# Loads and constants of an attention kernel's opening put in another order

## The chip, the cores and the metric

The kernel runs on one core of a Trainium2 chip. The metric is the device time of one execution in microseconds (us). Engines are named as the profile names them: PE is TensorE (PEld its weight loads), DVE is VectorE, ACT is ScalarE, POOL is GpSimd, SP is SyncE; SPq and ACTq are the queues on which SP and ACT issue transfers (DMAs).

## The reference: sparse attention, then two mixtures of experts

```python
scores = scale * np.matmul(q, k.transpose(0, 1, 3, 2))      # q, k, v: 2 x 8 heads x 576 x 64
kth = np.partition(scores, -top_k, axis=-1)[..., -top_k:-top_k + 1]      # top_k = 32
scores = np.where(scores >= kth, scores, -1e9)
attn = softmax(scores)
x = heads side by side of attn @ v                          # 1152 x 512
x = moe(x, w_gate, w1, w2, capacity)                        # 8 experts, 512 -> 1024 -> 512, best expert of each token
return moe2(x, w_gate, w1, w2)
```

## The kernel before: how the work is staged

Attention comes first and lasts to about 240 us; the two mixtures of experts follow. Attention works through eight units, each two heads of one batch, and each unit through nine tiles of 128 queries. For a tile PE makes the scores, ACT copies them to SBUF, and DVE looks for the 32nd largest score of each row (folds of maxima and minima, then MAX8 and MATCH_REPLACE8 in turn); then follow exponential and product with the values.

Products in full precision need each number in two parts. A unit's keys and queries are loaded (`kraw`, `qraw`), split into `ks` and `qs` (ACT copies the rounded part, DVE subtracts it from the raw number, POOL copies a third part of the keys), and turned by PE with a product against the identity matrix `identr`. For the first unit this is written out in `begin()`: the function `part_of` makes one copy and one subtraction, `whole` makes four transpositions, `wide_spin` and `spin` are products without use that keep PE busy. A unit's keys and queries have a main part (512 rows, as 128 partitions) and a tail (the last 64 rows). `begin()` asks for the main keys and queries of head 0, then both tails, then three groups of transpositions.

The identity matrices are made at the start of the kernel, in a block of constants: POOL writes a ramp `jp`, and DVE compares it with zero to give `ident`, `identr`, `negid`, `before` and `upto`. `coef` in the same block is a tile of three numbers; the first ACTIVATE of the kernel, on a tile `warm`, reads it and serves only to have ACT's function table loaded (ACT_TABLE_LOAD) early.

Each engine runs its own list of instructions in order. The block of constants and the attention are each written in an order by hand, but they are two blocks, and the builder merges them into one list for each engine: where a row of one stands beside rows of the other follows from the build. Waits between engines are semaphores set by the builder. Transfers are issued in order on SPq or ACTq.

Of the kernel before, what the change touches and what calls it, by code (L numbers as in the profile page):

```python
# [10 lines left out]
F32 = mybir.dt.float32  # L11
# [4 lines left out]
AF = mybir.ActivationFunctionType  # L16
# [9 lines left out]
BIG = 2.0 ** 80  # L26
# [28 lines left out]
def attn_moe_moe_kernel(ctx, tc, q, k, v, g1, w11, w12, capacity, g2, w21, w22, out):  # L55
    nc = tc.nc
    B, H, S, D = q.shape
# [4 lines left out]
    NC = (S + 127) // 128  # L62
    TAIL = S - (NC - 1) * 128
    cap = int(capacity)
    scale = 1.0 / math.sqrt(D)

    consts = ctx.enter_context(tc.tile_pool(name="consts", bufs=1))
    dram = ctx.enter_context(tc.tile_pool(name="dram", bufs=1, space=DR))
    first_w = ctx.enter_context(tc.tile_pool(name="mw1", bufs=1))

    with tc.manual_schedule():
        ones = consts.tile([128, 128], BF)
        nc.vector.memset(ones, 1.0)
        idle = consts.tile([128, 128], BF)
        nc.vector.memset(idle, 0.0)
        jp = consts.tile([128, 128], I32)
        nc.gpsimd.iota(jp, pattern=[[1, 128]], base=0, channel_multiplier=-1)
        ident = consts.tile([128, 128], F32)
        nc.vector.tensor_scalar(ident, jp, 0.0, None, op0=OP.is_equal)
        identr = consts.tile([128, 128], F32R)  # L80
        nc.vector.tensor_scalar(identr, jp, 0.0, None, op0=OP.is_equal)
        negid = consts.tile([128, 128], BF)
        nc.vector.tensor_scalar(negid, jp, 0.0, -1.0, op0=OP.is_equal, op1=OP.mult)
        coef = consts.tile([128, 3], F32)
        nc.vector.memset(coef[:, 0:1], -1.0)
        nc.vector.memset(coef[:, 1:2], BIG)
        nc.vector.memset(coef[:, 2:3], -scale)
        before = consts.tile([128, 128], BF)
        nc.vector.tensor_scalar(before, jp, 0.0, None, op0=OP.is_gt)
        upto = consts.tile([128, 128], BF)  # L90
        nc.vector.tensor_scalar(upto, jp, 0.0, None, op0=OP.is_ge)
# [100 lines left out]
    def attention():  # L192
# [4 lines left out]
        M = NC - 1  # L197
# [4 lines left out]
        with tc.tile_pool(name="ald", bufs=2) as ld, tc.tile_pool(name="awk", bufs=2) as wk, \  # L202
                tc.tile_pool(name="aps", bufs=1, space=PS) as ps, tc.manual_schedule():
            st = {}
            held_t = []
            for i in range(2):
                qt = wk.tile([128, 2, 192], F32R, name=f"qtail{i}", bufs=1)
                nc.gpsimd.memset(qt.bitcast(F32), 0.0)
                xl = wk.tile([128, NC, 2, XW], F32, name=f"xl{i}", bufs=1)
                vT = wk.tile([128, NC, 128], F32, name=f"vT{i}", bufs=1)  # L210
# [3 lines left out]
            shifted, under, vx = [], [], []  # L214
# [18 lines left out]
            xo = xb[:, :6 * XW].rearrange("p (g h w) -> p g h w", h=2, w=XW)  # L233
            zero = blank
            pend = []

            def load(u, what=("k", "q", "v"), eng=None):
                b, p = divmod(u, HP)
                z = st.setdefault(u, {"vT": held_t[u % 2][0], "xl": held_t[u % 2][1], "qtail": held_t[u % 2][2],
                                      "v": vx[u % 4]})  # L240
                dma = (eng or nc.sync).dma_start
                for nm in what:
                    s_ = {"k": k, "q": q, "v": v, "w": v}[nm][b, 2 * p:2 * p + 2]
                    if nm == "v":
                        if "vw" not in z:
                            load(u, ("w",))
                        for hh in range(2):
                            dma(z["v"][:, :M, hh, :D], s_[hh, :M * 128, :].rearrange("(s c) d -> s c d", s=128))
                        dma(z["v"][:TAIL, M, :, :D], s_[:, M * 128:, :].rearrange("h s d -> s h d"))
                    elif nm == "w":  # L250
                        t = z["vw"] = ld.tile([128, NC, 2, D], F32, name="vraw", bufs=2)
                        for hh in range(2):
                            dma(t[:, :M, hh], s_[hh, :M * 128, :].rearrange("(s c) d -> s c d", s=128))
                        dma(t[:TAIL, M], s_[:, M * 128:, :].rearrange("h s d -> s h d"))
                    else:
                        t = ld.tile([128, 2, NC, D], F32, name=nm + "raw", bufs=2)
                        if nm == "q":
                            for hh in range(2):
                                dma(t[:, hh, :M], s_[hh, :M * 128, :].rearrange("(c s) d -> s c d", s=128))
                        else:  # L260
                            dma(t[:, :, :M], s_[:, :M * 128, :].rearrange("h (s c) d -> s h c d", s=128))
                        dma(t[:TAIL, :, M], s_[:, M * 128:, :].rearrange("h s d -> s h d"))
                        z[nm] = t.rearrange("s h c d -> s c h d")
# [426 lines left out]
            def spin(n, o):  # L690
                for _ in range(n):
                    idle_product(o)
# [97 lines left out]
            seq = [(u, t) for u in range(NU) for t in order[u]]  # L790
            pairs = {}
            spin(17, xb[:, :256])
            load(0, ("k",))
            load(0, ("q",), nc.scalar)
            warm = wk.tile([128, 1], F32, name="warm", bufs=1)
            nc.scalar.activation(warm, coef[:, :1], AF.Exp)
            load(1, ("q",))
            load(0, ("w",))
            load(1, ("k",))
# [120 lines left out]
            for i in range(L - 4):  # L920
                k_, j_ = divmod(i, 2)
# [81 lines left out]
            z = st[u]  # L1003
# [13 lines left out]
            for c in range(NC):  # L1017
                w, k_ = c % 2, c // 2
# [1088 lines left out]
    rank_cuts = (0, 3, 6, 9, None)  # L2107
    w2_order = ((0, 1), (2, 3), (4, 5), (6, 7), (0, 1), (2,), (3, 4, 5, 6, 7))
    repair(attention())
    small = [ctx.enter_context(tc.tile_pool(name=f"msm{i}", bufs=1)) for i in range(2)]  # L2110
    onehot = small[0].tile([128, 128 * max(B * NC, NCOL + nov[0])], BF, name="onehot")
# [37 lines left out]
```

## Time and profile before

| | us |
|---|---|
| time before, median of 3 runs | 582.86 (582.47 to 583.42) |
| the profiled execution's own time | 583.19 |
| its span in the trace | 581.5 |
| PE busy | 566.0 (97%) |
| DVE busy | 475.5 (82%) |
| ACT busy | 419.4 (72%) |

The span is what the trace covers; 1.7 us of the execution's own time lie around it. The busy shares are means over stages with different limits: up to about 240 us DVE has no idle time to speak of, afterwards PE has none. "Idle before" in a row is the time that an engine stood still ahead of an instruction, with what ended it behind an arrow.

### The profile page before, as it was taken

The page shows a single profiled execution, that of the slowest core. Times are in us where ns is not written, and L with a number is a line of the kernel's source. Part 1 is how long each engine was busy: PE and PEld are TensorE (multiplying, and loading weights), DVE is VectorE, ACT ScalarE, POOL GpSimd, SP SyncE. Part 2 cuts the span into 40 slices and gives each one's busy share as a digit, 9 for nine tenths or more (in the row PEclk, how much of TensorE's full clock was granted, in tenths as well). Part 3 has the DMA queues.
Part 4 walks back from the last instruction along what each step waited for, and adds up shares of the span by engine and source line. Part 5 has one row for each costly group of instructions (what it writes and reads, how often), then busy time and mean ns, then how long its engine had stood idle before and what let it go on. Part 6 is the DMA issues. An engine that isn't in the chain of part 4 may idle for free. (4 is left out here: it accounts for less than half of the span.)

```text
span 581.5 us, 13994 instructions
## 1 busy us (share of the span) xinstructions
PE 566.0 (97%) x4786; PEld 539.2 (93%) x4786; DVE 475.5 (82%) x1588; ACT 419.4 (72%) x1040; POOL 267.1 (46%) x600
## 2 busy tenths in 40 slices
PE   8999999999999999989999999999999999999994
PEld 6799999999999999889999999998998899999993
DVE  6999999999999999868788788552588788889640
ACT  6789998999898988637687787452465677878550
POOL 8768888988898798546320111010103302220010
PEclk9999999999999999999999999999999999999998
DMA  6630513161211482055998767875777767678650
GB/s 145 143 83 2 169 46 114 45 127 43 70 48 62 70 254 77 23 196 181 349 280 282 221 227 250 287 236 198 237 253 244 278 232 260 225 249 298 211 203 14
DMA packets 85200, 100.76 MB, mean 173 GB/s; under 512 B 33957, under 2 KB 46757, under 8 KB 85120
## 3 DMA queue, kind: packets, MB, share of 16 engines
q1 hardware_dynamic: 79136, 86.69, 48.2%
q0 software_dynamic: 3728, 10.70, 5.4%
q10 hardware_dynamic: 2256, 2.39, 1.3%
q8 instruction: 40, 0.66, 0.5%
q14 instruction: 40, 0.33, 0.2%
HBM read 86.51 MB, written 13.74 MB: 172 GB/s over the span
## 5 line engine op out<-in xcount | busy, mean ns | idle before, releaser
L624 PE MATMUL xb<-vx,pT 128*128 128x73 f32 (+1 forms) x800 | 94.0, 266 | 0.2 <-ACT pT L1014 0.2
L1367 PE MATMUL pp<-xT,w1c 128*128 128x352 f32 (+4 forms) x316 | 92.4, 361 | 0.4 <-DVE xT L1323 0.4
L1288 DVE TENSOR_TENSOR w2c<-raw,w2c 128x512 fp32r<-128x512 f32 x112 | 74.5, 684 | 18.6 <-ACT w2c L1287 16.8
L624 PEld LDWEIGHTS xb<-vx,pT 128*128 128x128 f32 (+1 forms) x800 | 87.1, 181 | 2.5 <-issue 1.3
L1406 PE MATMUL pp<-hT,w2c 128*128 128x416 f32 (+4 forms) x320 | 88.7, 356 | 0.1
L1408 PE MATMUL pp<-hT,w2c 128*128 128x208 f32 (+4 forms) x320 | 77.8, 243 | 0.0
L1369 PE MATMUL pp<-xT,w1c 128*128 128x176 f32 (+4 forms) x316 | 77.0, 244 | 0.0
L1287 ACT ACTIVATE w2c<-raw 128x512 fp32r<-128x512 f32 x112 | 67.4, 624 | 8.7 <-PE pp L1408 3.7
L603 PE MATMUL pt<-ident,shifted 128*128 128x128 f32 x350 | 67.5, 278 | 0.0
L604 PE MATMUL pt<-negid,under 128*128 128x128 bf16 x350 | 63.5, 219 | 0.5 <-ACT under L594 0.5
L1288 DVE TENSOR_TENSOR w1c<-raw,w1c 128x512 fp32r<-128x512 f32 x88 | 55.9, 684 | 9.5 <-ACT w1c L1287 7.5
L1339 ACT ACTIVATE t<-pp 128x208 f32<-128x208 f32 (+4 forms) x120 | 37.6, 314 | 34.2 <-PE pp L1369 21.6
L1408 PEld LDWEIGHTS pp<-hT,w2c 128*128 128x128 f32 x320 | 61.0, 191 | 0.0
L1406 PEld LDWEIGHTS pp<-hT,w2c 128*128 128x128 f32 x320 | 60.0, 187 | 1.0 <-DVE hT L1333 0.8
L1367 PEld LDWEIGHTS pp<-xT,w1c 128*128 128x128 f32 x316 | 59.4, 188 | 1.4 <-DVE xT L1323 0.8
L1369 PEld LDWEIGHTS pp<-xT,w1c 128*128 128x128 f32 x316 | 60.4, 191 | 0.0
L1469 POOL DMA_INDIRECT out_dram<-yr,sidx x14 | 13.6, 972 | 101.1 <-ACT yr L1450 84.7
L594 ACT ACTIVATE under<-s,nb 128x576 bf16<-128x576 f32 x70 | 54.9, 786 | 1.5 <-POOL nb L586 1.3
L1792 POOL DMA_DIRECT2D y<-yr x13 | 7.6, 582 | 105.3 <-issue 45.1
L523 DVE MAX8 top<-ypair 128x8 f32<-128x160 f32 x192 | 54.7, 313 | 0.0
L597 POOL TENSOR_SCALAR shifted<-s,nb 128x576 f32<-128x576 f32 x70 | 52.3, 747 | 3.9
L603 PEld LDWEIGHTS pt<-ident,shifted 128*128 128x128 f32 x350 | 49.2, 140 | 3.6
(421 smaller groups left out, 1547.8 us busy)
## 6 DMA issues: line engine op xcount, KB each, us to landing
raw<-in_moe_w_dram SPq DMA_DIRECT2D x60, 1024.0 KB, 5.1
w1c<-in_moe_w_dram SPq DMA_DIRECT2D x8, 512.0 KB, 6.3
y<-blank SPq DMA_DIRECT2D x3, 769.5 KB
out_dram<-blank SPq DMA_DIRECT2D x3, 768.0 KB
y<-yr POOLq DMA_DIRECT2D x8, 256.5 KB
kraw<-in_k_dram SPq DMA_DIRECT2D x8, 256.0 KB, 3.4
vraw<-in_v_dram SPq DMA_DIRECT2D x16, 128.0 KB, 2.8
vx<-in_v_dram SPq DMA_DIRECT2D x16, 128.0 KB, 2.8
```

What stands on the lines that cost most here:

```text
L523: ops.append(lambda w=w, cur=cur: nc.vector.max(w, cur))
L594: nc.scalar.activation(under[k % 3][:, :S], s, AF.Relu, bias=nb[:, 1:2], scale=-BIG)
L597: nc.gpsimd.tensor_scalar(shifted[k % 3][:, :S], s, nb[:, 0:1], 1.0, op0=OP.add, op1=OP.mult)
L603: both = (nc.tensor.matmul(pt[:, o], shifted[k % 3][:, o], ident, is_transpose=True, start=True, stop=False), nc.tensor.matmul(pt[:, o], u ...
L604: nc.tensor.matmul(pt[:, o], under[k % 3][:, o], negid, start=False, stop=True))
L624: nc.tensor.matmul(o, pT[:, c2, cols], z["v"][:, c2, hh], start=(c2 == 0), stop=(c2 == NC - 1))
L1287: nc.scalar.activation(o[:, 0], src_, AF.Copy)
L1288: nc.vector.tensor_tensor(o[:, 1], src_, o[:, 0].bitcast(F32), op=OP.subtract)
L1367: nc.tensor.matmul(ph[:, :2 * n].rearrange("p (w n) -> p w n", w=2), w[f][:, 0, d], xT[:, d, :, :n], start=st, stop=False)
L1369: nc.tensor.matmul(ph[:, :n], w[f][:, 1, d], xT[:, d, 0, :n], start=False, stop=sp)
L1406: nc.tensor.matmul(py[:, :2 * n].rearrange("p (w n) -> p w n", w=2), w[f][:, 0, o], hT[:, f, :, :n], start=st, stop=False)
L1408: nc.tensor.matmul(py[:, :n], w[f][:, 1, o], hT[:, f, 0, :n], start=False, stop=sp)
```

## The change

Three things move. `coef` is written first in the block of constants. On ACT the function table's load stands behind one transfer's issue (the tail of the keys) in place of three (the queries of both heads and their tail). The first unit's transfers are shared out anew: SPq has the main keys, the main queries of head 0 and the tail of the queries, ACTq has the tail of the keys and, behind the table's load, the main queries of head 1.

```diff
     with tc.manual_schedule():
+        coef = consts.tile([128, 3], F32)
+        nc.vector.memset(coef[:, 0:1], -1.0)
+        nc.vector.memset(coef[:, 1:2], BIG)
+        nc.vector.memset(coef[:, 2:3], -scale)
         ones = consts.tile([128, 128], BF)
         nc.vector.memset(ones, 1.0)
...
         negid = consts.tile([128, 128], BF)
         nc.vector.tensor_scalar(negid, jp, 0.0, -1.0, op0=OP.is_equal, op1=OP.mult)
-        coef = consts.tile([128, 3], F32)
-        nc.vector.memset(coef[:, 0:1], -1.0)
-        nc.vector.memset(coef[:, 1:2], BIG)
-        nc.vector.memset(coef[:, 2:3], -scale)
...
+            def load_first(then):
+
+                z = st.setdefault(0, {"vT": held_t[0][0], "xl": held_t[0][1], "qtail": held_t[0][2], "v": vx[0]})
+                k_, q_ = k[0, :2], q[0, :2]
+                kt = ld.tile([128, 2, NC, D], F32, name="kraw", bufs=2)
+                qt = ld.tile([128, 2, NC, D], F32, name="qraw", bufs=2)
+                head = lambda hh: (qt[:, hh, :M], q_[hh, :M * 128, :].rearrange("(c s) d -> s c d", s=128))
+                tail = lambda t, s_: (t[:TAIL, :, M], s_[:, M * 128:, :].rearrange("h s d -> s h d"))
+                nc.sync.dma_start(kt[:, :, :M], k_[:, :M * 128, :].rearrange("h (s c) d -> s h c d", s=128))
+                nc.scalar.dma_start(*tail(kt, k_))
+                nc.sync.dma_start(*head(0))
+                then()
+                nc.sync.dma_start(*tail(qt, q_))
+                nc.scalar.dma_start(*head(1))
+                z["k"], z["q"] = (t.rearrange("s h c d -> s c h d") for t in (kt, qt))
...
-            load(0, ("k",))
-            load(0, ("q",), nc.scalar)
             warm = wk.tile([128, 1], F32, name="warm", bufs=1)
-            nc.scalar.activation(warm, coef[:, :1], AF.Exp)
+
+            def table_load():
+                nc.scalar.activation(warm, coef[:, :1], AF.Exp)
+
+            load_first(table_load)
             load(1, ("q",))
```

The built lists show more than the diff does. DVE's list of the kernel before, from the block of constants to the first unit's four first subtractions (128x4x64 is a main part of head 0, 64x2x64 a tail of both heads):

```order
L79 TENSOR_SCALAR ident<-jp 128x128
L81 TENSOR_SCALAR identr<-jp 128x128
L83 TENSOR_SCALAR negid<-jp 128x128
L85 MEMSET coef 128x1
L86 MEMSET coef 128x1
L87 MEMSET coef 128x1
L89 TENSOR_SCALAR before<-jp 128x128
L91 TENSOR_SCALAR upto<-jp 128x128
L717 TENSOR_TENSOR ks<-kraw,ks 128x4x64
L717 TENSOR_TENSOR qs<-qraw,qs 128x4x64
L717 TENSOR_TENSOR ks<-kraw,ks 64x2x64
L717 TENSOR_TENSOR qs<-qraw,qs 64x2x64
```

DVE's list of the changed kernel at the same place (its L733 is L717 of before):

```order
L75 MEMSET coef 128x1
L77 MEMSET ones 128x128
L79 MEMSET idle 128x64
L733 TENSOR_TENSOR ks<-kraw,ks 128x4x64
L733 TENSOR_TENSOR qs<-qraw,qs 128x4x64
L733 TENSOR_TENSOR ks<-kraw,ks 64x2x64
L733 TENSOR_TENSOR qs<-qraw,qs 64x2x64
L83 TENSOR_SCALAR ident<-jp 128x128
L85 TENSOR_SCALAR identr<-jp 128x128
L87 TENSOR_SCALAR negid<-jp 128x128
L89 TENSOR_SCALAR before<-jp 128x128
L91 TENSOR_SCALAR upto<-jp 128x128
```

The five comparisons that make `ident`, `identr`, `negid`, `before` and `upto` have moved from ahead of the four subtractions to behind them; no line of the diff says so.

ACT's list of the kernel before, from its first row:

```order
L259 DMA qraw<-in_q_dram 128x4x64 x2
L262 DMA qraw<-in_q_dram 64x2x64
L796 ACT_TABLE_LOAD
L796 ACTIVATE warm<-coef 128x1
L712 ACTIVATE ks<-kraw 128x4x64
L712 ACTIVATE qs<-qraw 128x4x64
L712 ACTIVATE ks<-kraw 64x2x64
L712 ACTIVATE qs<-qraw 64x2x64
```

ACT's list of the changed kernel at the same place:

```order
L246 DMA kraw<-in_k_dram 64x2x64
L812 ACT_TABLE_LOAD
L812 ACTIVATE warm<-coef 128x1
L250 DMA qraw<-in_q_dram 128x4x64
L728 ACTIVATE ks<-kraw 128x4x64
L728 ACTIVATE qs<-qraw 128x4x64
L728 ACTIVATE ks<-kraw 64x2x64
L728 ACTIVATE qs<-qraw 64x2x64
```

One issue stands ahead of the table's load where there were three, and one behind it. On SPq the list begins with the main keys in both kernels; before, the tail of the keys and unit 1's queries came next, and now two transfers of the first unit's queries stand ahead of unit 1's. PE's and POOL's lists keep their order.

## Rows read from the trace of the kernel before

**Rows 1.** Busy time by stretch: us, PE, PEld, DVE, ACT, POOL, granted clock, DMA.
```profile
0.00:10.00 10.00, 8.52 (x48) 6.04 (x48) 5.10 (x17) 5.63 (x14) 7.83 (x35) 1.00 0.74 150
10.00:20.00 10.00, 8.36 (x60) 6.36 (x60) 9.99 (x41) 6.94 (x16) 8.06 (x18) 1.00 0.66 154
...
180.00:200.00 20.00, 20.00 (x199) 19.26 (x198) 19.98 (x80) 18.49 (x46) 15.66 (x37) 1.00 0.47 95
...
300.00:400.00 100.00, 100.00 (x781) 97.37 (x780) 67.97 (x168) 64.56 (x165) 13.30 (x27) 1.00 0.79 253
```

**Rows 2.** DVE's waits, 9.6 to 60 us: total us, times, longest.
```profile
DVE hi L505 <- ACT s L478: 0.7, 2, 0.5
```

**Rows 3.** Timeline of DVE in the opening: start us, us, engine, line, operation.
```profile
1.26 0.41 DVE L79 TENSOR_SCALAR ident<-jp 128x128 f32<-128x128 int32 x1
1.40 0.34 DVE L81 TENSOR_SCALAR identr<-jp 128x128 fp32r<-128x128 int32 x1
...
4.54 0.43 DVE L717 TENSOR_TENSOR ks<-kraw,ks 128x256 fp32r<-128x256 f32 x1 [1.58 <-ACT ks L712]
...
6.22 0.28 DVE L717 TENSOR_TENSOR qs<-qraw,qs 64x128 fp32r<-64x128 f32 x1
...
9.60 0.31 DVE L505 TENSOR_TENSOR hi<-sc,s 128x144 f32<-128x144 f32 x1 [0.46 <-ACT s L478]
```

**Rows 4.** Timeline of PE in the opening.
```profile
1.25 3.79 PE L124 MATMUL xb<-idle,ones 128*128 128x256 bf16 x17 [1.25 <-DVE idle L75]
5.02 0.75 PE L285 MATMUL sc<-identr,ks 128*128 128x128 f32 x4
...
6.60 0.60 PE L124 MATMUL sc<-idle,ones 128*128 128x512 bf16 x2
7.14 0.25 PE L285 MATMUL xb<-identr,qs 64*128 64x64 f32 x1
...
8.27 0.54 PE L473 MATMUL pt<-qkT 128*128 128x288 f32 x2
```

**Rows 5.** Timeline of ACT in the opening.
```profile
0.85 1.07 ACTq L259 DMA_DIRECT2D qraw<-in_q_dram  x2
1.96 0.72 ACTq L262 DMA_DIRECT2D qraw<-in_q_dram  x1
2.71 1.28 ACT L796 ACT_TABLE_LOAD   x1 [2.71 <-issue]
4.00 0.20 ACT L796 ACTIVATE warm<-coef 128x1 f32<-128x1 f32 x1
4.11 0.40 ACT L712 ACTIVATE ks<-kraw 128x256 fp32r<-128x256 f32 x1
4.47 0.42 ACT L712 ACTIVATE qs<-qraw 128x256 fp32r<-128x256 f32 x1
5.45 0.31 ACT L712 ACTIVATE ks<-kraw 64x128 fp32r<-64x128 f32 x1 [0.56 <-DMA kraw<-in_k_dram]
5.72 0.31 ACT L712 ACTIVATE qs<-qraw 64x128 fp32r<-64x128 f32 x1
```

**Rows 6.** Timeline of SP's queue in the opening.
```profile
0.86 0.44 SPq L261 DMA_DIRECT2D kraw<-in_k_dram  x1
1.36 0.75 SPq L262 DMA_DIRECT2D kraw<-in_k_dram  x1
2.15 1.34 SPq L259 DMA_DIRECT2D qraw<-in_q_dram  x2
```

**Rows 7.** DMA issues, 0 to 30 us: KB each, median us from issue to landing.
```profile
qraw<-in_q_dram SPq DMA_DIRECT2D x6, 128.0 KB, 3.3
...
wg<-in_moe_w_gate_dram SPq DMA_DIRECT2D x2, 16.0 KB, 2.2
```

**Rows 8.** PE's products by shape in short stretches: count, busy us, mean ns.
```profile
L124 PE MATMUL xb<-idle,ones 128*128 128x256 bf16 x10 | 2.3, 421 | 0.0
...
L124 PE MATMUL sc<-idle,ones 128*128 128x512 bf16 x4 | 1.0, 382 | 0.0
```

## The prediction

> **What bounds the kernel now.** I read the busy time by stretch first [rows 1]. From 10 us on DVE is busy 9.99 of 10 us, and at 180 to 200 us still 19.98 of 20; from 300 us it is PE, 100 of 100. Between 0 and 10 us no engine is full: DVE has 5.10 us of work there. DVE's waits say the same: from 9.6 to 60 us it stands still for 0.7 us in all, and 0.46 of that is the wait for its very first fold [rows 2, 3]. So the opening is a chain of latencies that ends when DVE's first fold begins at 9.60, and after that DVE runs without a gap. Whatever moves 9.60 moves the rest of attention by the same amount, and what follows waits for attention's end.
>
> Second, the chain itself, followed back from 9.60. The fold waits for ACT's copies of the first scores; the scores start at 8.27 [rows 4]. Back from there PE has hardly a gap: tails turned from 7.14, idle products from 6.60, and the first transpositions from 5.02. These start 0.05 us after DVE's first subtraction (4.54 + 0.43 = 4.97) [rows 3], which waits for ACT's copy at 4.11, and that begins as soon as the table is loaded (2.71 to 3.99) and the small ACTIVATE on it is done [rows 5]. The 17 idle products fill PE from 1.25 to 5.04, so it has no gap. The identity is long there: `identr` ends at 1.40 + 0.34 = 1.74 [rows 3].
>
> **The change, part by part.** *The table's load.* ACT issues one tail in place of three transfers: 0.85 + 0.72 = 1.57, table from 1.60 to 2.88, small ACTIVATE to 3.09, then the queries of head 1 (half of 1.07, 0.54) to about 3.64. The first copy can start at 3.66 and not 4.11 [rows 5]: a gain of 0.45 us, if the keys have landed; before shows only that they had at 4.11, so the gain is between 0 and 0.45. `coef` written earlier costs nothing: it stands under ACT's issue and the load.
>
> *The identity.* This is what decides. DVE runs its list in order, and in the changed list `ident` and `identr` stand behind all four subtractions, the tails' too. PE's first transposition needs `identr`. So PE no longer waits for the first subtraction but for: the tail of the queries landed, ACT's copy of it, DVE's subtraction, two comparisons. I work it out from the start of ACT's copy of that tail, X. The subtraction follows 0.34 later (copy 0.31 and 0.03 from copy's end to subtraction, as 4.51 to 4.54) and takes 0.28 [rows 3, 5]. `ident` to the end of `identr` takes 1.74 - 1.26 = 0.48, and PE starts 0.05 after DVE. Together X + 1.15.
>
> X has two bounds. ACT makes three copies first: from 3.66 the steps of before (4.11 to 4.47 is 0.36; 0.42 less an overlap, 0.33; 5.45 to 5.72 is 0.27) give 4.62. And the tail must land. On SPq it is now third: keys 0.86 to 1.30, queries of head 0 from 1.36 for half of 1.34, so its issue starts at about 2.05 [rows 6]. From issue to landing the nearest rows are 2.2 us (gate weights, in a quiet stretch), 3.3 (median of unit 1's and later queries) [rows 7], and, in this very stretch, the tail of the keys: issued at 1.36, it kept ACT waiting until 5.45, that is 4.09 [rows 5, 6]. So it lands at 4.25, 5.35 or 6.14, and X is 4.62, 5.35 or 6.14. I take the middle: it has only the keys and one head of queries ahead of it on its queue, but the opening's transfers overlap as before. PE then starts at 5.77, 6.50 or 7.29 in place of 5.02: **+0.75, +1.5 or +2.3 us**.
>
> For the tail of the keys the wait of 0.56 on ACT shows what is at stake. A rule of the Trainium skill speaks to it ("DMA: Bandwidth & Descriptors", section "Issuing engines are not separate DMA queues"): transfers issued from different engines run on the same DMA engines and interleave, so that another issuer saves issue time alone. By this rule the landings would not get earlier, the tail of the queries would take what the tail of the keys took, and the sum would be its upper end, +2.3; no run here shows yet whether it holds.
>
> Behind the late start everything keeps its distance: PE's list from 5.02 to 8.27 is the same and is full, ACT's first copy of a turned block needs PE, and DVE's other comparisons (three more, done about 1.2 us after `identr`) end before the next DVE row needs its data. Unit 1's transfers move back by about 0.6 us on SPq; POOL's and ACT's work on them has the same delay of everything else as cover.
>
> *PE's clock.* The granted clock reads 1.00 throughout [rows 1], but the products tell two levels: a 256-column product takes 421 ns before 5 us and a 512-column product 382 ns later [rows 8], which is 1.2 and 2.4 GHz. The rise comes near 6.5 us, after more than five us without a pause. In the changed kernel PE stops at 5.04 and stands still for about 1.5 us. If the clock is up by then all the same, the twelve transpositions of 128 columns each save 128/1.2 - 128/2.4 = 53 ns, -0.6 us. If the rise is put off beyond the first scores, five idle products of 512 columns cost 0.21 us more each, four score products of 288 columns 0.12, six of 64 columns 0.03: +1.7. I take +0.3, nearer to no change, since there are two ways.
>
> **Sum.** +1.5 + 0.3 = +1.8 us on the span of 581.5, so 583.3, and with the 1.7 around it 585.0 for a profiled execution of the kind of 583.19. That execution lies 0.33 above the median of the runs; on the median it is 582.86 + 1.8 = **584.7**. A measurement of this kernel can tell about 0.2%, 1.17 us, from no change; the forecast lies above that, not by much.
>
> **The rivals.** *A. The loads come early and the wait is covered (same).* If the tail of the queries lands by 5.0, that is under 3.0 us after its issue, PE starts at 6.15 at the latest, +1.13 or less: no measurable difference, 583.0 to 584.0. For it: 2.2 and 3.3 are rows, and ACTq carries 32 KB in place of 288 at first. Against it: the 4.09 of the tail of the keys. The point from which it decides is 5.0. Chance 0.22.
>
> *B. The clock's rise is put off (slower still).* The pause ahead of the first transposition costs PE its higher clock until after the first scores: +1.5 + 1.7 = +3.2, 586.1. For it: the rise came only after a long unbroken stretch, and now there is a pause right ahead of it. Against it: the pause is short, and 17 products stand ahead. "TensorE: Matmul & The Clock Gate" of the Trainium skill, in "Part 1: The HAM clock gate", says that the clock goes up after sustained activity and that the moment shifts from run to run; by this, both ways would be seen in different executions. Chance 0.20.
>
> *C. The earlier table decides (not slower).* The 0.45 us come through in full and the identity is not waited for. It is -0.45, 582.4, and even so inside 0.2%. Against it is DVE's list: an engine cannot pass over the rows ahead of `ident`. Chance 0.05.
>
> **How the numbers follow.** The forecast, PE late by the queries' tail, +1.2 to +2.4, has 0.53; B 0.20, A 0.22, C 0.05. The ends of the terms are +0.75 - 0.6 = +0.15 and +2.3 + 1.7 = +4.0; eight in ten lie between +0.5 and +3.6: 583.3 to 586.4. Slower by over 0.2% are the forecast and B, 0.73 less 0.02 for its lower edge: 0.71. Same: A, C and that edge less 0.03: 0.26. Faster 0.03, by drift alone, since no mechanism here reaches 1.17 us.
>
> **What the profile of the changed kernel would show.** Right: the table's load starts near 1.6 and the first copy on ACT before 4.1; DVE's `identr` stands behind a subtraction of 64x128 at 6.0 to 6.5; PE has an idle gap between its 17 idle products and the first transposition, released by DVE's `identr`, and that starts at 5.8 to 7.3; the first fold starts later than 9.60 by as much, and the later stages have their lengths of before. Wrong: `identr` done before 5 us (the list is not what runs), or a first fold that moves by less than PE's start (slack that I did not see), or an attention that ends no later although its first fold does.

## The result and the profile after

The changed kernel takes 586.77 us (median of 6 runs, 585.63 to 587.78) against 582.88 for before (6 runs): a ratio of 1.007, 95% interval 1.006 to 1.008, so 3.5 to 4.7 us slower. The forecast was slower, 584.7, with a range up to 586.4: the direction held, the size did not. The profiled execution is the fastest of the six, 585.63 with a span of 583.8, so its trace shows the lower end of the loss, +2.3 us on the span.

Busy time of the changed kernel by stretch, columns as in [rows 1]:

```profile
0.00:10.00 10.00, 6.91 (x39) 4.67 (x40) 3.40 (x15) 4.33 (x10) 7.59 (x35) 0.92 0.72 151
10.00:20.00 10.00, 8.29 (x52) 6.35 (x51) 7.86 (x32) 6.84 (x18) 8.23 (x18) 0.91 0.65 149
...
180.00:200.00 20.00, 20.00 (x203) 19.42 (x202) 19.96 (x82) 17.65 (x44) 16.13 (x37) 1.00 0.46 95
```

The loss arises in the first two rows. DVE has 3.40 and 7.86 us of work there in place of 5.10 and 9.99, 3.8 us less; from 180 to 200 us it is as busy as before. Not all of the 3.8 is loss: the comparisons are also shorter at their new place (`ident` and `identr`, below, take 0.21 us each, 0.41 and 0.34 before). And the granted clock, 1.00 before, reads 0.92 and 0.91.

Timeline of ACT in the changed kernel's opening, which answers to [rows 5]:

```profile
0.87 0.71 ACTq L246 DMA_DIRECT2D kraw<-in_k_dram  x1
1.61 1.28 ACT L812 ACT_TABLE_LOAD   x1 [1.61 <-PEq L2150]
1.68 0.54 ACTq L250 DMA_DIRECT2D qraw<-in_q_dram  x1
...
4.00 0.42 ACT L728 ACTIVATE ks<-kraw 128x256 fp32r<-128x256 f32 x1 [0.89 <-DMA kraw<-in_k_dram]
4.75 0.42 ACT L728 ACTIVATE qs<-qraw 128x256 fp32r<-128x256 f32 x1 [0.34 <-DMA qraw<-in_q_dram]
5.08 0.29 ACT L728 ACTIVATE ks<-kraw 64x128 fp32r<-64x128 f32 x1
5.65 0.31 ACT L728 ACTIVATE qs<-qraw 64x128 fp32r<-64x128 f32 x1 [0.28 <-DMA qraw<-in_q_dram]
```

The table is loaded 1.10 us earlier, and 0.11 of that is left at the first copy: ACT now waits 0.89 us for the keys themselves. The queries of head 0 are copied 0.28 later than before, the tail of both heads' queries at 5.65 (5.72 before). So the copy that `identr` now stands behind is no later than it was.

Timeline of DVE in the changed kernel, which answers to [rows 3]:

```profile
6.18 0.27 DVE L733 TENSOR_TENSOR qs<-qraw,qs 64x128 fp32r<-64x128 f32 x1
6.38 0.21 DVE L83 TENSOR_SCALAR ident<-jp 128x128 f32<-128x128 int32 x1
6.51 0.21 DVE L85 TENSOR_SCALAR identr<-jp 128x128 fp32r<-128x128 int32 x1
...
12.47 0.31 DVE L521 TENSOR_TENSOR hi<-sc,s 128x144 f32<-128x144 f32 x1 [1.62 <-ACT s L494]
```

Timeline of PE in the same stretch, which answers to [rows 4]:

```profile
1.34 3.79 PE L124 MATMUL xb<-idle,ones 128*128 128x256 bf16 x17 [1.34 <-DVE idle L79]
6.87 0.51 PE L301 MATMUL sc<-identr,ks 128*128 128x128 f32 x4 [1.74 <-DVE identr L85]
...
9.59 1.46 PE L124 MATMUL sc<-idle,ones 128*128 128x512 bf16 x3
10.49 1.04 PE L489 MATMUL pt<-qkT 128*128 128x288 f32 x2
```

PE's first transposition waits 1.74 us and is released by `identr`: it starts at 6.87 in place of 5.02, 1.85 late. Four transpositions then take 0.51 in place of 0.75, so PE is at its higher clock; but three idle products of 512 columns, further on, take 1.46 (0.82 before), and two score products 1.04 in place of 0.54. The first fold begins at 12.47 in place of 9.60, 2.87 late: 1.85 by the start and 1.0 between.

PE in short stretches of the same trace (us, PE, PEld, DVE, ACT, POOL, granted clock, DMA):

```profile
6.87:8.00 1.13, 1.13 (x12) 1.13 (x13) 0.49 (x3) 0.58 (x1) 1.01 (x2) 1.00 0.74 153
8.00:8.50 0.50, 0.50 (x3) 0.10 (x1) 0.46 (x1) 0.41 (x2) 0.50 (x1) 0.91 0.78 205
...
9.00:11.50 2.50, 2.50 (x12) 1.80 (x12) 0.43 (x1) 0.69 (x2) 1.85 (x6) 0.50 0.58 92
11.50:12.50 1.00, 0.95 (x6) 0.63 (x5) 0.03 (x1) 0.89 (x3) 1.00 (x1) 0.84 0.61 136
```

By the granted clock of these stretches it falls to 0.50 (1.2 GHz) near 8.4, when PE has been busy again for 1.5 us, and is back at 1.00 (2.4 GHz) near 11.8. Before that PE had stood still from 5.13 to 6.87.

### The profile page after: what moved, and what is told of

Same layout as the page of the kernel before. It is cut to its first block, busy times and chain, and to the rows that moved or that the text cites. A ratio compares the mean times of both kernels' runs of the same rounds, so it can differ in the third digit from the quotient of the medians.

```text
span 583.8 us, 13995 instructions
## 1 busy us (share of the span) xinstructions
PE 567.0 (97%) x4786; PEld 540.1 (93%) x4786; DVE 474.8 (81%) x1588; ACT 419.0 (72%) x1040; POOL 266.1 (46%) x600
## 4 chain that ended last, share of the span: by engine, by line
PE 39%; DMA 9%; issue 5%; DVE 1%; POOLq 0%; POOL 0%; ACT 0%; DVEq 0%; ACTq 0%
PE pp L1385 8%; DMA out_dram<-yr,sidx 8%; PE pp L1424 8%; PE pp L1387 4%; PE pp L1371 3%; PE pp L1426 3%; PE pl L1438 2%; PE pt L1335 2%; PE pt L1475 1%; PE pp L1877 1%; PE pp L1420 1%; PE pp L1422 1%; PE pp L1421 1%; DMA xr<-y,gid 1%; PE pp L1374 1%
```

## The experiments

The theory after the result had two parts: `identr` behind the four subtractions starts PE late, and the pause that this leaves behind the idle products costs PE its clock. The rivals were that the new order of the transfers costs the time, and that the late start alone does. Each run is compared with before on its own chip (583.83 for the first four, 583.51 for the last four).

**The loads alone.** `coef` is put back where it was; the rest of the change stays.

```diff
-        coef = consts.tile([128, 3], F32)
-        nc.vector.memset(coef[:, 0:1], -1.0)
...
         ones = consts.tile([128, 128], BF)
...
         nc.vector.tensor_scalar(negid, jp, 0.0, -1.0, op0=OP.is_equal, op1=OP.mult)
+        coef = consts.tile([128, 3], F32)
+        nc.vector.memset(coef[:, 0:1], -1.0)
...
```

> The new transfers and the table's load behind one issue, but coef written where it was before, so that DVE's list has the identity ahead of the subtractions again. Theory (the identity's place costs the time): PE's first transposition starts near 4.95 again, without a pause behind the idle products, and the time is that of before within 0.5 us (582.4 to 583.4). Rival (the new order of the transfers costs it): the queries' tail and head 0 land late here too, and most of the 3.9 us stays (585.5 to 587).

Measured: 589.1, ratio 1.0094 (1.0079 to 1.0109). Neither theory nor rival had this: 5.3 us slower, worse than the whole change. ACT's timeline in this run:

```profile
7.03 0.42 ACTq L250 DMA_DIRECT2D qraw<-in_q_dram  x1
7.49 0.42 ACT L728 ACTIVATE ks<-kraw 128x256 fp32r<-128x256 f32 x1 [4.39 <-DMA vraw<-in_v_dram]
```

PE's first transpositions in the same trace:

```profile
8.43 0.75 PE L301 MATMUL sc<-identr,ks 128*128 128x128 f32 x4 [3.39 <-DVE ks L733]
```

The identity is early again, but ACT stands for 4.39 us ahead of the issue of head 1's queries, until a transfer of the first unit's values, `vraw`, has landed. The built list says why: transfers carry one of eight semaphores in turn, and in this build head 1's queries came ninth and had to wait for the one that held their semaphore.

```
L250 DMA qraw_179<-in_q_dram 128x4x64 [waits DMAHW7_49]
```

In the changed kernel the same row has no wait. So this run does not tell the theories apart; the run with two issues, below, does.

**`coef` alone.** The kernel before with `coef` written first; transfers and the table's load as before.

```diff
+        coef = consts.tile([128, 3], F32)
+        nc.vector.memset(coef[:, 0:1], -1.0)
...
         ones = consts.tile([128, 128], BF)
...
         nc.vector.tensor_scalar(negid, jp, 0.0, -1.0, op0=OP.is_equal, op1=OP.mult)
-        coef = consts.tile([128, 3], F32)
-        nc.vector.memset(coef[:, 0:1], -1.0)
...
```

> Only coef is written first; transfers and table's load as before. DVE's list has the identity behind the four subtractions. Theory: ACT copies the queries' tail at 5.7 as before, so identr ends near 6.8, PE starts near 6.9 after a pause of 1.8 us, and the time is that of the changed kernel or a little more (586 to 588). Rival (the transfers cost it): as before, 582.9.

Measured: 587.2, ratio 1.006 (1.0044 to 1.0075), 3.4 us slower. PE's timeline in this run:

```profile
7.08 0.55 PE L285 MATMUL sc<-identr,ks 128*128 128x128 f32 x4 [2.45 <-DVE identr L85]
7.43 0.71 PE L285 MATMUL pg<-identr,qs 128*128 128x128 f32 x4
```

Four lines that write three constants, and touch no transfer, cost about what the whole change costs (3.4 and 3.9 us): in DVE's list they put the identity behind the subtractions. Here the pause is 2.45 us, and the clock falls inside the first transpositions: the first four take 0.55, the next four 0.71.

**The pause filled.** The changed kernel with more idle products, so that PE does not stand still.

```diff
-            spin(17, xb[:, :256])
+            spin(25, xb[:, :256])
```

> The changed kernel with 25 idle products of 256 columns ahead of the first transposition in place of 17, so that PE is busy through most of its pause; identity as late as in the changed kernel. Theory (two costs: late start, and the clock that the pause takes away): PE's first transposition still near 6.9, but the granted clock stays at 1.00 through the first scores, the first fold starts near 11 and the time is 584.0 to 584.8. Rival (the late start alone, the clock costs nothing of note): as the changed kernel, 586 to 587.

Measured: 585.41, ratio 1.0028 (1.0016 to 1.0039), 1.6 us slower than before. The time lies above the 584.0 to 584.8 that were expected, but before is 0.9 us slower on this chip than the 582.9 that the expectation went by; the loss is the expected one. PE's timeline:

```profile
1.34 5.49 PE L124 MATMUL xb<-idle,ones 128*128 128x256 bf16 x25 [1.34 <-DVE idle L79]
6.68 0.72 PE L301 MATMUL sc<-identr,ks 128*128 128x128 f32 x4
...
9.76 0.54 PE L489 MATMUL pt<-qkT 128*128 128x288 f32 x2
```

The first fold on DVE and the subtraction behind it:

```profile
11.08 0.31 DVE L521 TENSOR_TENSOR hi<-sc,s 128x144 f32<-128x144 f32 x1 [0.61 <-ACT s L494]
...
11.72 1.43 DVE L732 TENSOR_TENSOR qs<-qraw,qs 128x256 fp32r<-128x256 f32 x1
```

POOL beside it:

```profile
11.59 1.28 POOL L290 TENSOR_TENSOR ks<-kraw,ks 128x512 fp32r<-128x512 f32 x1
```

The same subtraction in the kernel before:

```profile
10.24 0.42 DVE L716 TENSOR_TENSOR qs<-qraw,qs 128x256 fp32r<-128x256 f32 x1
```

PE starts 1.66 late, much as without the filling (1.85, and 1.67 in a second trace), but two score products take 0.54 again and the first fold is only 1.48 late. More useless work on PE takes back more than half of the loss: the late start alone is not the cause of all of it. The 1.6 us that stay are not the late start alone either, as far as this trace goes, which is of the slowest of the six executions (586.33). In it DVE's subtraction behind the first fold takes 1.43 us in place of 0.42, beside a row of POOL; it takes 1.03 and 1.16 in the traces of the next two runs, and 0.43 and 0.48 in the two of the changed kernel. How often this happens in executions without a trace is not known.

**The pause alone.** The kernel before with fewer idle products; identity and first transposition stay early.

```diff
-            spin(17, xb[:, :256])
+            spin(9, xb[:, :256])
```

> The kernel before with 9 idle products in place of 17: identity, transfers and PE's first transposition stay at 5.02, but PE stands still from about 3.3 to 5.0. Theory: the pause alone costs clock in the opening, 0.50 granted or a later rise over some 3 us, and the time is 584 to 585.5. Rival (a pause without a late start costs nothing): 582.9 within 0.5 us.

Measured: 586.83, ratio 1.0053 (1.0039 to 1.0067), 3.1 us slower, more than was expected. PE's timeline:

```profile
5.02 0.75 PE L285 MATMUL sc<-identr,ks 128*128 128x128 f32 x4 [1.70 <-DVE ks L717]
...
6.62 1.08 PE L124 MATMUL sc<-idle,ones 128*128 128x512 bf16 x2
...
9.40 1.04 PE L473 MATMUL pt<-qkT 128*128 128x288 f32 x2
...
15.66 1.04 PE L473 MATMUL pt<-qkT 128*128 128x288 f32 x2
...
17.85 0.47 PE L473 MATMUL sc<-qkT 128*128 128x288 f32 x2
```

Nothing but useless products was taken away, the first transposition starts at 5.02 to the hundredth, and the loss is that of most of the change. Two score products take 1.04 at 9.40 and still at 15.66, where before they take 0.54 [rows 4]: PE keeps its lower clock until nearly 18 us. In the changed kernel the clock had risen and fell; here it does not rise until then.

DVE's folds that wait for scores in the same trace:

```profile
11.41 0.31 DVE L505 TENSOR_TENSOR hi<-sc,s 128x144 f32<-128x144 f32 x1 [1.41 <-ACT s L478]
...
18.83 0.46 DVE L505 TENSOR_TENSOR hi<-sc,s 128x288 f32<-128x288 f32 x1 [0.81 <-ACT s L478]
...
24.48 0.46 DVE L505 TENSOR_TENSOR hi<-sc,s 128x288 f32<-128x288 f32 x1 [0.50 <-ACT s L478]
```

The first fold is 1.81 late, and behind it DVE waits for scores twice more.

**Half of the pause.** As the last, with 13 products.

```diff
-            spin(17, xb[:, :256])
+            spin(13, xb[:, :256])
```

> The kernel before with 13 idle products in place of 17: PE stands still for about 0.85 us ahead of its first transposition, half of the pause of the run with 9. Theory (it is the pause that costs, and the longer the more often): PE's first transposition at 5.02, a longer stretch at the lower clock than before in part of the executions, +0.5 to +2 us. Rival (a pause of under a microsecond is free): before within 0.5 us.

Measured: 584.97, ratio 1.0024 (1.0015 to 1.0033), 1.5 us slower. PE's timeline:

```profile
5.03 0.75 PE L285 MATMUL sc<-identr,ks 128*128 128x128 f32 x4 [0.85 <-DVE ks L717]
...
9.48 1.04 PE L473 MATMUL pt<-qkT 128*128 128x288 f32 x2
10.32 0.47 PE L473 MATMUL sc<-qkT 128*128 128x288 f32 x2
```

A pause of 0.85 us is not free; here the rise comes near 10.4.

**The identity on POOL.** The changed kernel, `ident` and `identr` written by POOL behind the ramp.

```diff
-        nc.vector.tensor_scalar(ident, jp, 0.0, None, op0=OP.is_equal)
+        nc.gpsimd.tensor_scalar(ident, jp, 0.0, 1.0, op0=OP.is_equal, op1=OP.mult)
...
-        nc.vector.tensor_scalar(identr, jp, 0.0, None, op0=OP.is_equal)
+        nc.gpsimd.tensor_scalar(identr, jp, 0.0, 1.0, op0=OP.is_equal, op1=OP.mult)
```

> The changed kernel, with ident and identr written by POOL right behind the ramp in place of DVE; transfers, table and coef as changed, negid, before and upto still behind the subtractions on DVE. Theory (the identity's place is the cause, by its wait and by PE's pause): identr is done near 2 us, PE's first transposition starts at 4.9 to 5.1 without a pause, and the time is that of before within 0.6 us. Rival (the transfers' new order also costs): the second group of transpositions waits for head 0's queries (copied at 4.75 in place of 4.47) and 1 us or more stays.

Measured: 583.78, ratio 1.0005 (0.9996 to 1.0014): no difference from before. PE's first transpositions:

```profile
5.02 0.72 PE L301 MATMUL sc<-identr,ks 128*128 128x128 f32 x4
```

POOL's row for `identr`:

```profile
2.22 0.63 POOL L85 TENSOR_SCALAR identr<-jp 128x128 fp32r<-128x128 int32 x1
```

Transfers, table and `coef` are those of the change, and the whole loss is gone. The identity's place is the cause.

**Two issues.** `coef` back, and the queries of head 1 issued ahead of the table's load, which takes away the wait of the run with the loads alone.

```diff
...
-                then()
                 nc.sync.dma_start(*tail(qt, q_))
                 nc.scalar.dma_start(*head(1))
+                then()
```

> coef where it was before, the new transfers, but the queries of head 1 issued ahead of the table's load (two issues ahead of it in place of one or three), which takes them out of the wait for the eighth earlier transfer that held ACT until 7.0 in the run with the loads alone. Theory: identity early, table from 2.2 to 3.5, keys copied at 4.0 as they land, PE from 4.9; the time is that of before within 0.6 us. Rival (the new transfers themselves cost, and the run with the loads alone showed it): 585.5 or more.

Measured: 583.42, ratio 1.0001 (0.9989 to 1.0014); one of its 12 executions, without a trace, took 587.16. ACT's first copy:

```profile
3.93 0.42 ACT L728 ACTIVATE ks<-kraw 128x256 fp32r<-128x256 f32 x1 [0.18 <-DMA kraw<-in_k_dram]
```

PE's first transpositions:

```profile
4.86 0.75 PE L301 MATMUL sc<-identr,ks 128*128 128x128 f32 x4
```

The new transfers with an early identity start PE 0.16 us earlier than before, which no timing of this kernel can tell. None of the versions beats the kernel before.

**The changed kernel again**, for a second trace.

> The changed kernel once more, for a second trace. Theory (the time of an execution goes with the length of the stretch at the lower clock behind the pause): another execution shows another stretch, 3 to 7 us, and its span goes with it. Rival: the same stretch from 8.4 to 11.7, whatever the span.

Measured: 587.09 (2 runs), ratio 1.0061 (1.0044 to 1.0079); the profiled one took 588.0 with a span of 586.1. PE's first transpositions:

```profile
6.69 0.51 PE L301 MATMUL sc<-identr,ks 128*128 128x128 f32 x4 [1.57 <-DVE identr L85]
```

PE in stretches (us, PE busy, granted clock, DMA):

```profile
8.00:9.00 1.00, 1.00 (x8) 0.82 0.78 235
9.00:10.00 1.00, 1.00 (x4) 0.50 0.66 65
...
18.00:19.00 1.00, 1.00 (x5) 0.56 1.06 242
```

DVE's waits from 9 to 40 us:

```profile
DVE hi L521 <- ACT s L494: 3.3, 3, 1.7
```

The first transposition starts 0.18 earlier than in the other trace, and the first fold at 12.08, 0.39 earlier. Yet the execution is 2.4 us longer: the lower clock lasts from 8.6 to 18.9, 10.2 us where 3 to 7 were expected and the other trace has 3.4, and DVE waits three times for scores, 3.3 us in all, where the other trace has one wait of 1.6. Two traces are few, but the span went with the stretch, as the theory has it.

## Why the prediction was wrong in its size

*Where the time is decided.* Right in the main. The loss arises in the opening and is carried through attention. The operation of DVE that ends attention, in the kernel before (the number behind the durations is the first start):

```profile
L915 DVE SCALAR_TENSOR_TENSOR kraw<-s,top,lo x2: 817/817/817, 240.5 to 241.6; 128x576 f32<-128x576 f32 x2
```

In the changed kernel:

```profile
L933 DVE SCALAR_TENSOR_TENSOR kraw<-s,top,lo x2: 818/819/820, 243.6 to 244.8; 128x576 f32<-128x576 f32 x2
```

In its second trace:

```profile
L933 DVE SCALAR_TENSOR_TENSOR kraw<-s,top,lo x2: 818/818/819, 245.4 to 246.5; 128x576 f32<-128x576 f32 x2
```

That is +3.1 and +4.9, with spans +2.3 and +4.6; what takes the difference off behind attention is not shown. One part of the step was too narrow: the opening does not end at the first fold. In the second trace DVE waited for scores twice more behind it. And the first fold did not move by as much as PE's start, as was forecast, but by 1.0 and 0.8 more.

*The identity's place.* Right, and shown: with the identity on POOL the loss vanishes, with `coef` alone it appears. The term was +1.5 within +0.75 to +2.3; the two traces have +1.85 and +1.67. The copy of the queries' tail starts at 5.65 (5.35 forecast) and `identr` releases PE 1.22 later (1.15 forecast). With the pause filled, 1.6 us of loss are left.

*PE's clock.* This is the step that failed: "I take +0.3, nearer to no change, since there are two ways", and the end of +1.7 for a rise put off "beyond the first scores". The pause alone, with nothing late, costs 3.1 us, half of the pause 1.5. In the changed kernel's two traces attention ends 3.1 and 4.9 later, and PE starts 1.85 and 1.67 late; the rest, 1.2 and 3.2 us, is a difference and no measured price, but it stands where the +0.3 stood. Two things were wrong. The choice between the two ways held a pause of about 1.5 us (1.74 and 1.57 in the traces) to be short, against the 17 products ahead of it; and the upper end was priced only up to the first scores. So far it was fair (the pause alone moved the first fold by 1.81), but the lower clock lasted to 11.8 in one trace of the changed kernel, to 18.9 in another, and to nearly 18 with the pause alone, and DVE went on waiting. In both traces the clock was even up at PE's late start, as in the favourable way, and fell near 8.4 and 8.6 behind the pause, which neither way had. The levels themselves were read rightly, though the durations of single products do not give them: 17 products of 256 columns in 3.79 us are 223 ns each, 1.15 columns a ns, near the 1.2 GHz of the lower level, and not 421. Rival B, with 0.20 and 586.1, was the nearest of the cases and still 0.7 short. The two costs, 1.6 and 3.1, add up to 4.7 where the change measures 3.9: they do not simply add up. A late start at the higher clock (0.51 in place of 0.75 for four transpositions) gives a little back, and both of these runs' traces have the long subtraction beside POOL, which the changed kernel's have not; no run tells the two reasons apart.

The two traces of the changed kernel have the fall at 8.4 and 8.6 and the rise behind it at 11.8 and 18.9. The page "TensorE: Matmul & The Clock Gate" of the Trainium skill, in "Part 1: The HAM clock gate", has the moment at which the clock goes up vary from run to run. The two traces agree that it varies.

*The table's load.* Forecast as a gain of 0 to 0.45, measured 0.11 at the first copy, since the keys landed at 4.00. Rival C is out: the run with two issues has the table early, the identity early and no gain. Shared out anew, the transfers landed the keys at 4.00 (by 4.11 before, where ACT did not wait for them) and head 0's queries at 4.75 (by 4.47 before), and with the identity early the time is that of before. The rule of the Trainium skill in "DMA: Bandwidth & Descriptors", section "Issuing engines are not separate DMA queues", has another issuer save issue time alone. Nothing in these rows speaks against it, but the +2.3 that the prediction drew from it did not come: the tail of the queries took 3.8 us and not the 4.09 of the tail of the keys.

*The tail and rival A.* SPq's row for the queries' tail in the changed kernel:

```profile
1.86 0.75 SPq L249 DMA_DIRECT2D qraw<-in_q_dram  x1
```

It was issued at 1.86 and waited for until 5.65, 3.8 us, between the 3.3 and 4.09 of the rows; A's point of 5.0 was passed. That 5.35 came near was in part luck: the issue was taken 0.2 too late and the transfer 0.5 too short, and the two errors partly offset each other.

## What to carry to other kernels

Read the built list of each engine, not the diff: four lines that write three constants earlier moved five others behind a wait for a transfer, and in another build the same transfers ran into a reused semaphore. When a kernel keeps TensorE busy with idle products ahead of its first real work, their number is part of the schedule: work that then starts later, or fewer products, left a pause here whose cost was not its length but the stretch at the lower clock behind it. Price such a pause up to the point where the engine that bounds the stage stops waiting, not to its first instruction.

## What the runs showed of the hardware that was not expected

The clock was up at PE's first transposition at 6.87 and fell 1.5 us later, while PE was busy; what went ahead of the fall is the pause from 5.13 to 6.87. A pause of 0.85 us ahead of real work cost 1.5 us, one of 1.70 cost 3.1.

The record of the granted clock does not show a lower level that an execution starts in. With the pause alone it reads 1.00 while the products of 512 columns take 1.08 us for two:

```profile
5.00:8.00 3.00, 2.98 (x17) 1.00 0.92 180
```

The durations of products of one shape tell the level there, 1.04 against 0.54 us for two score products.

ACT's queue issued a transfer at 1.68 while ACT loaded its table from 1.61 to 2.89, so an issue written behind the load did not wait for it; the forecast had it at 3.1.

One and the same subtraction on DVE (`qs`, 128x256) took 0.42 us in the kernel before. Where it started inside a row of POOL of 1.28 us it took 1.43, 1.16 and 1.03 (with 25, 13 and 9 idle products) and 0.48 (the changed kernel's second trace), and each time it ended 0.27 or 0.28 us behind that row. So a chain that starts later can meet another engine's work that it was clear of before. That POOL's row is the cause is not shown by a run of its own.
